# Mean square of x from each head's 32x32 matrix of v_m with itself, summed by VectorE's accumulating product, with another seed for the planner

## The chip, the cores and the metric

The kernel runs on one core of one Trainium2 chip. The metric is the device time of one execution in microseconds (us), as the median of the runs. A profiled execution gives the trace from which rows are quoted.

## The reference, cut to what matters

Three stages run one after the other on inputs of 4 batches, 8 heads, 576 positions and 64 columns per head: an attention through 32 memory slots per head, a gated feed-forward layer behind an RMS norm, and a second feed-forward layer.

```python
a = softmax(phi, axis=2)                              # over the 576 positions; phi: 4,8,576,32
k_m = einsum('bhsm,bhsd->bhmd', a, k)                 # 32x64 per head
v_m = einsum('bhsm,bhsd->bhmd', a, v)
attn = softmax(q @ k_m.T / 8, axis=-1)                # 576x32 per head
x = (attn @ v_m) with the heads side by side          # 2304 x 512
rms = sqrt(mean(x * x, axis=-1) + 1e-6)
xn = x / rms * rms_g
h = silu(xn @ w_gate) * (xn @ w_val)                  # d_ff 1536
x2 = h @ w_out
out = gate(x2 @ w_in) @ w_out2                        # d_ff 2048
```

q and k are 200 times their usual size, so the scores are far apart. The weights come as float64 and are converted to float32 on the chip.

## The kernel before, in words

The kernel never forms xn. It multiplies v_m (with the gains rms_g folded in, tile `vT`) into the gate and value weights, 128 rows of weights per chunk (`chunk`, `convert`, `vw`), and applies the scaled attention weights A = attn / rms to the product (`gv`). What it needs of x is only its mean square per token, for 1 / rms.

The attention part goes by batch and by pair of token blocks:

- `soft(b)` makes the exponentials of phi, `memory(b)` forms k_m and v_m of a batch on TensorE (tile `kvps`), divides by the sums (tiles `kd`, `vs`), transposes both into one PSUM bank (`kT`), and copies out `kmT` (ScalarE) and `vT` (VectorE).
- `spread_v(b)` lays v_m out as `vbd`: for each group of 4 heads a 128 x 256 matrix with the 32 x 64 block of each head on its diagonal.
- `pair(n)` runs 10 times: eight pairs of two blocks of 128 tokens (I = 2), and two rest pairs with 64 tokens of each of two batches (I = 1). It forms the scores (`sc`), the softmax (`mx`, `e`, `sm`), transposes the weights (`aTp`, copied to `aT`), multiplies them by `vbd` to get x itself in PSUM (`xp`, L844, one bank for each i), and ScalarE squares and sums x (`square`, L835). GpSimd turns the sum into 1 / rms (L856, L860) and scales the weights (L862), which are transposed (`ATp`, L870) and split into a high and a low part (`Ah`, `Al`, or in `late`).

Then `gv` makes the products with the weights (`gps`, `vps`, L984), `gate` the activation, `out1` the first layer's output (L1079), `quads` and `outs` the second layer (L1423, L1546).

The order of all instructions is fixed when the program is built. `Agenda` plays the kernel's generators against assumed costs (`yield "V", 0.45` is 0.45 us on VectorE), always starts what can start first, and breaks ties by priority. A `yield` with two engine letters lets it pick the engine that would end first: `"VAhi"` and `"VAsign"` in the weight conversion (VectorE or ScalarE), `"VGvbd"` in `spread_v` (VectorE or GpSimd). Costs are wobbled by up to 3% with a random generator that starts from `SEED`, so another seed gives another order throughout the program. `heat` puts idle matmuls of zeros (`heat`, L586) where TensorE would have nothing to do, until k_m of batch 3 is there.

Of the kernel before, what the change touches and what calls it, by code (L numbers as in the profile page):

```python
# [9 lines left out]
F32 = mybir.dt.float32  # L10
# [3 lines left out]
AF = mybir.ActivationFunctionType  # L14
ALU = mybir.AluOpType
AX = mybir.AxisListType
P = 128
# [8 lines left out]
BUFS = {"phi": 2, "kv": 2, "q": 2, "qr": 2, "pm": 1, "gm": 2, "s1": 2, "kd": 2, "qT": 2, "e": 4, "aT": 3, "half": 1, "raw": 4, "x": 2, "w": 2, "vw": 2, "ab": 3, "tx": 6, "w2s": 2, "wr": 8, "u": 6, "gs": 20, "gg": 6, "uo0": 5, "uo1": 5}  # L26
# [18 lines left out]
DUTY = {"Pm": 0.64, "Pw": 0.83, "Ps": 0.5}  # L45
W_AFTER = [("km", 0)]
WO1_AFTER = {(0, 0): ('gv', 8), (1, 0): ('gv', 12), (0, 1): ('gv', 9), (1, 1): ('gv', 12), (0, 2): ('gv', 10), (1, 2): ('gv', 12), (0, 3): ('gv', 11), (1, 3): ('gv', 12), (0, 4): ('gv', 12), (1, 4): ('gv', 12), (0, 5): ('gv', 13), (1, 5): ('gv', 12)}
BIAS = {"VAhi": -0.0664, "GAlow": -0.8, "VGlo": 0.3, "GVe": 0.8, "VGal": 0.3, "VAsign": 0.5, "VGvbd": -0.169, "VAgate": 0}
DMA_LAG = 1.8
D_HALF = 1.7  # L50
OVER = {"V": 0.085, "A": 0.1}
FETCH = (256, 63, 80.0, 6.1, 3.6, 80)
TICK = 3.413
SEED, WOBBLE = 4, 0.06
WARM = 1.38
P_SOFT, P_PAIR, P_CONV, P_VW, P_GV, P_OUT1, P_W2, P_F2 = 0, 100, 800, 102, 850, 900, 3000, 4000
P_W = 4004
# [9 lines left out]
class Agenda:  # L67
# [28 lines left out]
    def add(self, pri, stream):  # L96
        self.count += 1
        self._go([pri, self.count, stream, None, self.done, ""], None)
# [131 lines left out]
def tile_attn_moe(tc, q, k, v, phi, w_gate, w_val, w_out1, rms_g, w_in2, w_out2, out):  # L230
# [10 lines left out]
    nc = tc.nc  # L241
    B, H, S, D = q.shape
    M = phi.shape[3]
    DM = H * D
# [6 lines left out]
    HP = P // 2  # L251
# [5 lines left out]
    HM = H * M  # L257
# [21 lines left out]
    def bank(tag, name):  # L279

        early = BANKS.get(tag + "0") if "attention" not in agenda.flags else None
        z = yield "pick", early or BANKS[tag]
        return psum.tile([P, 512], F32, tag=f"b{z}", name=name), ("bank", z)
# [4 lines left out]
    mask, half, ones, power = consts[:, 0:4], consts[:, 4:5], consts[:, 5:6], consts[:, 6:8]  # L288
# [12 lines left out]
    vT = [keep.tile([P, KC, M], F32, name=f"vT{b}") for b in range(B)]  # L301
# [5 lines left out]
    add, mark = agenda.add, agenda.set  # L307
# [117 lines left out]
    st = pool(att, "st", "right")  # L425
# [1 line left out]
    rest, th_free, th_home = [], [], []  # L427
    qr_t = {}
    kmT_t = [st.tile([P, H, 2, M], F32, name=f"kmT{b}") for b in range(B)]
    vbd_t = [st.tile([P, 2, 4, D], F32, name=f"vbd{b}") for b in range(B)]  # L430
    gT = st.tile([P, KC], F32, name="gT")
    g4 = st.tile([KC, P], F32, name="g4")
    nc.scalar.dma_start(out=g4, in_=rms_g.rearrange("(c p) -> c p", p=P))
# [160 lines left out]
    def memory(b):  # L594
# [6 lines left out]
        for j in range(J):  # L601
            yield "Pm32", 0.22
            for g in range(2):
                gs = slice(HP * g, HP * g + HP)
# [56 lines left out]
                tp[:, P * g : P * g + P], kd[:, g].rearrange("p t d -> p (t d)"), ident  # L661
            )
        nc.tensor.transpose(tp[:, HM : HM + P], vs.rearrange("p g d -> p (g d)"), ident)
        add(P_SOFT + 2 * b + 1, spread_v(b, vs))
        kmT = kmT_t[b]
        for z in range(2):
            yield "A", 0.38
# [9 lines left out]
            out=vT[b], in0=tp[:, HM : HM + P].rearrange("p (c m) -> p c m", c=KC),  # L677
            in1=gT.unsqueeze(2).to_broadcast([P, KC, M]), op=ALU.mult,
        )
        yield "give", tp_bank  # L680
        mark(("vT", b))

    def spread_v(b, vs):
        vbd = vbd_t[b]
        for g in range(2):
            eng = yield "VGvbd", (0.41, 0.62)
            (nc.vector if eng == "V" else nc.gpsimd).tensor_tensor(
                out=vbd[:, g],
                in0=vs[:, g].unsqueeze(1).to_broadcast([P, 4, D]),
                in1=mask.unsqueeze(2).to_broadcast([P, 4, D]),  # L690
                op=ALU.mult,
            )
        mark(("vbd", b))
        yield "give", "kd"

    def used_q(b):
# [44 lines left out]
    def per_batch(pr):  # L741
        if pr[0] == B:
            return [(b, slice(HP * k, HP * k + HP)) for k, b in enumerate(RESTS[pr[1]])]
        return [(pr[0], slice(0, P))]

    def pair(n):
# [80 lines left out]
        nc.scalar.activation(out=aT, in_=tv, func=AF.Copy)  # L827
        yield "give", tp_bank
        for bb, _ in per_batch(pr):
            yield "flag", ("vbd", bb)  # L830
        ss = st.tile([P, I], F32, tag="ss", name=f"ss_{name}", bufs=BUFS["e"])

        def square(i, xp, x_bank):
            yield "A", 0.78
            nc.scalar.activation(out=xp, in_=xp, func=AF.Square, accum_out=ss[:, i : i + 1])  # L835
            yield "give", x_bank
            mark(("ss", pr, i))

        for i in range(I):
            xp, x_bank = yield from bank("x", f"xp_{name}_{i}")  # L840
            yield f"P{8 * len(per_batch(pr))}", 0.86
            for g in range(2):
                for bb, rows in per_batch(pr):
                    nc.tensor.matmul(  # L844
                        out=xp[rows, 256 * g : 256 * g + 256],
                        lhsT=aT[:, i, g, rows],
                        rhs=vbd_t[bb][:, g].rearrange("p h d -> p (h d)"),
                        start=True, stop=True, skip_group_check=True,
                    )
            add(pri, square(i, xp, x_bank))  # L850
        yield "give", "aT"
        for i in range(I):
            yield "flag", ("ss", pr, i)
        y = st.tile([P, I], F32, tag="y", name=f"y_{name}", bufs=BUFS["e"])
        yield "G", 0.3
        nc.gpsimd.tensor_scalar(  # L856
            out=y, in0=ss, scalar1=1.0 / DM, scalar2=1e-6, op0=ALU.mult, op1=ALU.add
        )
        yield "G", 0.72
        nc.gpsimd.tensor_tensor(out=y, in0=y, in1=power[:, 0:I], op=ALU.pow)  # L860
# [808 lines left out]
```

## Time and profile before

| | |
|---|---|
| median of the runs | 773.75 us |
| profiled execution | 773.81 us |
| its span, first to last instruction | 772.0 us |
| TensorE matmul busy | 759.0 us (98%) |
| VectorE (DVE) busy | 621.6 us (81%) |
| ScalarE (ACT) busy | 462.7 us (60%) |
| GpSimd (POOL) busy | 61.1 us (8%) |

Busy time is the union of an engine's instructions; the rest of the span the engine waits. "PEld" are TensorE's weight loads, which overlap its matmuls. A float32 matmul of the program is two matmul instructions in the trace. Shares over the whole span hide that the attention part, in the first 94 us, loads the engines quite differently from the rest.

### The profile page before, as it was taken

Reading aid. Unit: us, or ns where it says so; the run is one execution under the profiler, and the core shown is the slowest. Engines: PE = TensorE matmul, PEld = TensorE weight load, DVE = VectorE, ACT = ScalarE, POOL = GpSimd, SP = SyncE. Lnnn points to the kernel's source line nnn. Section 1 sums busy time; section 2 is a strip of 40 time slices with the busy share of each in tenths; the row PEclk is TensorE's granted clock in tenths of the full one; section 3 lists DMA queues with packets and bytes.
Section 4 is the critical chain, followed back from the end, with each engine's and each line's share of the span. In section 5 each row is a group of like instructions: output and inputs, shape, how many; then the busy total and the mean of one; then the engine's idle time right before and its main releaser. Section 6 shows DMA issues by size and latency. Waiting matters only on the chain.

```text
span 772.0 us, 17234 instructions
## 1 busy us (share of the span) xinstructions
PE 759.0 (98%) x6383; PEld 700.6 (91%) x6383; DVE 621.6 (81%) x1257; ACT 462.7 (60%) x959; POOL 61.1 (8%) x84
## 2 busy tenths in 40 slices
PE   8899999999999999999999999999999999999997
PEld 4678888889999888988899999999999999999997
DVE  5798889998877787756789889997789895589963
ACT  2688887755556555645566656564467463565552
POOL 1556610000001000000000000000000000000000
PEclk9999999999999999999999999999999999999999
DMA  9995535788779775599647999779888878757866
GB/s 343 377 385 160 199 111 188 258 275 270 253 237 305 251 248 187 205 324 324 208 168 219 326 305 305 252 249 318 293 251 262 296 241 258 254 182 251 270 217 209
DMA packets 113371, 197.49 MB, mean 256 GB/s; under 512 B 10372, under 2 KB 41096, under 8 KB 113288
## 3 DMA queue, kind: packets, MB, share of 16 engines
q1 hardware_dynamic: 112368, 194.88, 75.4%
q10 hardware_dynamic: 920, 1.51, 0.5%
q8 instruction: 51, 0.84, 0.4%
q14 instruction: 32, 0.26, 0.1%
HBM read 151.26 MB, written 45.09 MB: 254 GB/s over the span
## 4 chain that ended last, share of the span: by engine, by line
PE 92%; DVE 3%; DMA 2%; ACT 1%; issue 1%; ACTq 0%; SPq 0%; DVEq 0%
PE ops L1079 18%; PE acc_b L1546 17%; PE qb L1423 12%; PE gps L984 10%; PE vps L984 10%; PE qc L1423 6%; PE acc_c L1546 6%; PE qa L1423 3%; PE vwps L934 3%; PE xp L844 2%; DMA kv<-in_k_dram 1%; PE kvps L606 1%; PE sc L723 1%; PE qps L772 1%; DMA x1B<-x_d 1%
## 5 line engine op out<-in xcount | busy, mean ns | idle before, releaser
L1079 PE MATMUL ops<-ab,wo1h 128*128 128x512 f32 (+1 forms) x480 | 137.2, 371 | 0.5 <-ACT xs L1093 0.5
L1423 PE MATMUL qb<-xop,wr 128*128 128x384 f32 x576 | 111.7, 337 | 0.0
L1423 PEld LDWEIGHTS qb<-xop,wr 128*128 128x128 f32 x576 | 100.3, 187 | 0.9 <-DVE xop L1298 0.5
L1079 PEld LDWEIGHTS ops<-ab,wo1h 128*128 128x128 f32 x480 | 84.7, 189 | 15.8 <-issue 2.9
L1079 PE MATMUL ops<-ab,wo1l 128*128 128x512 f32 (+1 forms) x240 | 88.4, 368 | 0.0
L1546 PE MATMUL acc_b<-wor,gg_A 128*128 128x256 f32 x648 | 80.8, 280 | 1.0 <-ACT gg_A L1494 0.8
L1546 PEld LDWEIGHTS acc_b<-wor,gg_A 128*128 128x128 f32 x648 | 79.3, 188 | 1.3 <-ACT gg_A L1494 1.0
L1385 ACT ACTIVATE u<-qb 128x384 f32<-128x384 f32 x72 | 35.2, 489 | 49.7 <-PE qb L1423 49.1
L1423 PE MATMUL qc<-xop,wr 128*128 128x384 f32 x288 | 58.3, 337 | 0.0
L1546 PE MATMUL acc_c<-wor,gg_S 128*128 128x256 f32 x432 | 53.0, 279 | 0.0
L1079 PEld LDWEIGHTS ops<-ab,wo1l 128*128 128x128 f32 x240 | 45.2, 188 | 7.9
L1546 PEld LDWEIGHTS acc_c<-wor,gg_S 128*128 128x128 f32 x432 | 52.2, 188 | 0.0
L1546 PE MATMUL acc_b<-wor,gg_S 128*128 128x256 f32 x432 | 51.7, 279 | 0.0
L1546 PEld LDWEIGHTS acc_b<-wor,gg_S 128*128 128x128 f32 x432 | 51.3, 188 | 0.0
L1423 PEld LDWEIGHTS qc<-xop,wr 128*128 128x128 f32 x288 | 50.9, 187 | 0.0
L344 ACT ACTIVATE raw<-raw 128x512 uint32<-128x512 uint32 x68 | 45.3, 673 | 0.0
L1016 ACT ACTIVATE kvth<-gps 128x64 f32<-128x64 f32 (+2 forms) x101 | 28.9, 305 | 18.8 <-PE gps L984 18.5
L984 PE MATMUL gps<-late,vwh 128*128 128x288 f32 x192 | 39.6, 294 | 0.0
L984 PE MATMUL vps<-late,vwh 128*128 128x288 f32 x192 | 39.6, 294 | 0.0
L1050 ACT ACTIVATE ab<-kvth 128x512 fp32r<-128x512 f32 (+1 forms) x40 | 22.7, 566 | 26.1 <-PE ops L1079 26.1
L954 DVE TENSOR_TENSOR vwl<-vwps,vwh 128x512 fp32r<-128x512 f32 x48 | 32.3, 685 | 7.2 <-ACT vwh L952 6.9
L1494 ACT ACTIVATE gg_S<-gs 128x384 fp32r<-128x384 f32 x52 | 26.8, 522 | 17.5 <-PE acc_b L1546 8.5
(188 smaller groups left out, 1730.1 us busy)
## 6 DMA issues: line engine op xcount, KB each, us to landing
wr<-win_d SPq DMA_DIRECT2D x168, 256.0 KB, 4.0
wor<-wout_d SPq DMA_DIRECT2D x168, 256.0 KB, 3.3
raw<-in_moe_w_out_dram SPq DMA_DIRECT2D x28, 512.0 KB, 4.9
win_d<-wins SPq DMA_DIRECT2D x56, 256.0 KB, 2.8
wout_d<-wouts SPq DMA_DIRECT2D x56, 256.0 KB, 2.9
raw<-in_moe_w_in_dram SPq DMA_DIRECT2D x16, 512.0 KB, 4.9
raw<-in_moe_w_gate_dram SPq DMA_DIRECT2D x12, 512.0 KB, 4.8
raw<-in_moe_w_val_dram SPq DMA_DIRECT2D x12, 512.0 KB, 5.7
```

The costliest lines, as they stand in the source:

```text
L344: nc.scalar.activation(out=low, in_=low, func=AF.Copy, scale=LOW_SCALE, bias=LOW_BIAS)
L844: nc.tensor.matmul(out=xp[rows, 256 * g : 256 * g + 256], lhsT=aT[:, i, g, rows], rhs=vbd_t[bb][:, g].rearrange("p h d -> p (h d)"), start ...
L934: nc.tensor.matmul(out=vps[g][0][32 * c : 32 * c + 32, 2 * P * x : 2 * P * x + 2 * P], lhsT=vT[n // NF1 * 2 + x][hs, c, :], rhs=t[hs, c].r ...
L954: nc.vector.tensor_tensor(out=lv, in0=vps[g][0], in1=hv.bitcast(F32), op=ALU.subtract)
L984: nc.tensor.matmul(out=p[:, 0:HB], lhsT=wt[:, g, i, :], rhs=at[b][:, g, c], start=(g == 0 and y == 0), stop=(g == 1 and y == 2),)
L1016: nc.scalar.activation(out=t, in_=g[:, c], func=AF.Silu)
L1050: nc.scalar.activation(out=ah, in_=src, func=AF.Copy)
L1079: nc.tensor.matmul(out=p[:, 0:n], lhsT=wt[:, fc, d], rhs=at, start=(fc == 0 and x == 0), stop=(fc == NF1 - 1 and x == 2),)
L1385: nc.scalar.activation(out=u, in_=src, func=AF.Copy)
L1423: nc.tensor.matmul(out=bank, lhsT=wt[:, kc, :], rhs=xt[:, kc, :], start=(start and kc == 0 and i == 0), stop=(kc == 1 and i == 2), skip_gr ...
L1494: nc.scalar.activation(out=t[:, 0], in_=src, func=AF.Copy)
L1546: nc.tensor.matmul(out=acc[x + "001"[t]][:, t % 2], lhsT=g[:, gi, P * t : P * t + P], rhs=w[:, wi], start=((o, t) in FIRST and q == 0 and ...
```

## The change

The product with `vbd`, and the square of x, go. In their place `memory` copies the transposed v_m of a batch (`vsT`) out of PSUM on ScalarE, and `gram` multiplies it with itself: for each group of 4 heads a 128 x 128 matrix, of which a mask keeps the 32 x 32 block of each head (`gram_t`). `pair` multiplies the transposed weights by it (`zp`, 128 columns in place of 256, both i in one PSUM bank), and VectorE multiplies the result with the weights themselves, 256 columns for each i, and sums along the row (`accum_out`); the sum over d of x squared is a G a for G = v_m v_m'. GpSimd's first step clips at zero and adds 1e-6. `"VGvbd"` leaves the planner's list, and SEED goes from 4 to 12.

```diff
-BIAS = {"VAhi": -0.0664, ..., "VGvbd": -0.169, "VAgate": 0}
+BIAS = {"VAhi": -0.0664, ..., "VAgate": 0}
-SEED, WOBBLE = 4, 0.06
+SEED, WOBBLE = 12, 0.06
-    vbd_t = [st.tile([P, 2, 4, D], F32, name=f"vbd{b}") for b in range(B)]
+    gram_t = [st.tile([P, 2, 4, M], F32, name=f"gram{b}") for b in range(B)]
@@ memory
-        add(P_SOFT + 2 * b + 1, spread_v(b, vs))
...
+        mark(("vT", b))
+        yield "A", 0.25
+        vsT = st.tile([P, P], F32, tag="vsT", name=f"vsT{b}", bufs=BUFS["kd"])
+        nc.scalar.activation(out=vsT, in_=tp[:, HM : HM + P], func=AF.Copy)
         yield "give", tp_bank
-        mark(("vT", b))
+        add(P_SOFT + 2 * b + 1, gram(b, vsT))
-    def spread_v(b, vs):
...
+    def gram(b, vsT):
+        gp = []
         for g in range(2):
-            eng = yield "VGvbd", (0.41, 0.62)
-            (nc.vector if eng == "V" else nc.gpsimd).tensor_tensor(
-                out=vbd[:, g], in0=vs[:, g]..., in1=mask..., op=ALU.mult)
-        mark(("vbd", b))
+            gp.append((yield from bank("t", f"gramps{b}_{g}")))
+        yield "P8", 0.6
+        for g in range(2):
+            gs = slice(HP * g, HP * g + HP)
+            nc.tensor.matmul(out=gp[g][0][:, 0:P], lhsT=vsT[gs], rhs=vsT[gs], start=True, stop=True, ...)
+        for g in range(2):
+            yield "V", 0.29
+            nc.vector.tensor_tensor(
+                out=gram_t[b][:, g], in0=gp[g][0][:, 0:P].rearrange("p (h m) -> p h m", h=4),
+                in1=mask.unsqueeze(2).to_broadcast([P, 4, M]), op=ALU.mult)
+            yield "give", gp[g][1]
+        mark(("gram", b))
         yield "give", "kd"
@@ pair
-            yield "flag", ("vbd", bb)
+            yield "flag", ("gram", bb)
-        def square(i, xp, x_bank):
-            yield "A", 0.78
-            nc.scalar.activation(out=xp, in_=xp, func=AF.Square, accum_out=ss[:, i : i + 1])
-            yield "give", x_bank
-            mark(("ss", pr, i))
+        zp, z_bank = yield from bank("x", f"zp_{name}")
+        yield f"P{8 * I * len(per_batch(pr))}", 0.96 * w * len(per_batch(pr))
         for i in range(I):
-            xp, x_bank = yield from bank("x", f"xp_{name}_{i}")
-            yield f"P{8 * len(per_batch(pr))}", 0.86
             for g in range(2):
                 for bb, rows in per_batch(pr):
                     nc.tensor.matmul(
-                        out=xp[rows, 256 * g : 256 * g + 256],
+                        out=zp[rows, 256 * i + P * g : 256 * i + P * g + P],
                         lhsT=aT[:, i, g, rows],
-                        rhs=vbd_t[bb][:, g].rearrange("p h d -> p (h d)"),
+                        rhs=gram_t[bb][:, g].rearrange("p h m -> p (h m)"),
                         start=True, stop=True, skip_group_check=True)
-            add(pri, square(i, xp, x_bank))
         yield "give", "aT"
+        zv = zp[:, 0 : I * HM].rearrange("p (t n) -> p t n", t=I)
         for i in range(I):
-            yield "flag", ("ss", pr, i)
+            yield "V", 0.45
+            nc.vector.scalar_tensor_tensor(
+                out=zv[:, i], in0=zv[:, i], scalar=1.0 / DM, in1=ev[:, i],
+                op0=ALU.mult, op1=ALU.mult, accum_out=ss[:, i : i + 1])
+        yield "give", z_bank
-        yield "G", 0.3
-        ... scalar1=1.0 / DM, scalar2=1e-6, op0=ALU.mult, op1=ALU.add
+        yield "G", 0.4
+        ... scalar1=0.0, scalar2=1e-6, op0=ALU.max, op1=ALU.add
```

## Rows read from the trace of the kernel before

**Rows 1.** The page: busy time, share and instructions of each engine; the chain by engine.

```profile
PE 759.0 (98%) x6383; PEld 700.6 (91%) x6383; DVE 621.6 (81%) x1257; ACT 462.7 (60%) x959; POOL 61.1 (8%) x84
...
PE 92%; DVE 3%; DMA 2%; ACT 1%; issue 1%; ACTq 0%; SPq 0%; DVEq 0%
```

**Rows 2.** Busy time by stretch (us from the start; its length, then engines as headed).

```profile
core 0: us, PE busy (x) PEld busy (x) DVE busy (x) ACT busy (x) POOL busy (x), PEclk, DMA share, GB/s
...
28.00:88.00 60.00, 56.70 (x875) 46.06 (x874) 52.87 (x113) 53.22 (x116) 40.12 (x48) 1.00 0.75 260
88.00:330.00 242.00, 242.00 (x2126) 215.65 (x2125) 199.85 (x427) 153.09 (x353) 11.74 (x11) 1.00 0.69 236
330.00:690.00 360.00, 358.90 (x2293) 346.67 (x2292) 290.87 (x553) 208.64 (x402) 1.53 (x1) 1.00 0.81 267
690.00:768.20 78.20, 77.32 (x649) 76.94 (x647) 60.46 (x121) 38.81 (x78) 0.00 (x0) 1.00 0.74 235
```

**Rows 3.** Busy time by stretch of the zero matmuls at L586 alone (PE, PEld).

```profile
28.00:88.00 60.00, 1.14 (x3) 0.35 (x3) 1.00 0.75 260
```

**Rows 4.** Line 984, first gate product: min/median/max ns, first and last start.

```profile
L984 PE MATMUL gps<-Ah,vwh x96: 288/295/402, 65.9 to 189.5; 128*128 128x288 f32 x96
```

**Rows 5.** Instructions on tile `q`, loads to landing included.

```profile
L493 SPq DMA_DIRECT2D q<-in_q_dram x4: 373/679/2121, 2.3 to 43.8; - x4
...
DMA to landing us min/median/max: 9.8/12.8/13.0
```

**Rows 6.** Tile `xp`: its instructions, min/median/max ns, first and last start.

```profile
L844 PEld LDWEIGHTS xp<-vbd,aT x80: 133/190/192, 28.0 to 86.4; 128*128 128x128 f32 x64, 128*64 128x64 f32 x16
L844 PE MATMUL xp<-vbd,aT x80: 379/379/483, 28.1 to 86.6; 128*128 128x256 f32 x64, 128*64 128x256 f32 x16
L835 ACT ACTIVATE xp<-xp x18: 582/590/603, 29.2 to 87.5; 128x512 f32<-128x512 f32 x18
L835 ACT ACTIVATION_READ_ACCUMULATOR xp<-xp x18: 181/194/202, 29.7 to 88.0; 128x1 f32 x18
```

**Rows 7.** The chain that ended last: start us, us, what.

```profile
32.50 1.92 PE xp L844 x8
...
40.03 0.44 PE ATp L870 x4
...
60.92 1.01 PE xp L844 x8
...
759.64 8.49 PE acc_b L1546 x72
```

**Rows 8.** The page's costliest groups: a weight load of the last stage.

```profile
L1546 PEld LDWEIGHTS acc_b<-wor,gg_A 128*128 128x128 f32 x648 | 79.3, 188 | 1.3 <-ACT gg_A L1494 1.0
```

**Rows 9.** Busy time by stretch of the matmuls at L844 alone (PE).

```profile
28.00:65.90 37.90, 9.29 (x40) 1.00 0.89 315
```

**Rows 10.** Busy time over 36 to 54 us, the sum of three 6-us stretches.

```profile
sum 18.00, PE 16.27 PEld 12.84 DVE 17.42 ACT 15.38 POOL 11.55; mean PE 5.42 PEld 4.28 DVE 5.81 ACT 5.13 POOL 3.85
```

**Rows 11.** Groups by form, 0 to 110 us, ACT: a 128-column copy from PSUM.

```profile
L881 ACT ACTIVATE Ah<-ATp 128x128 fp32r<-128x128 f32 x2 | 0.5, 272 | 0.0
```

**Rows 12.** Groups by form, 0 to 110 us, DVE: busy us, mean ns; idle before.

```profile
L954 DVE TENSOR_TENSOR vwl<-vwps,vwh 128x512 fp32r<-128x512 f32 x10 | 6.7, 680 | 1.7 <-ACT vwh L952 1.5
L355 DVE SCALAR_TENSOR_TENSOR w<-raw,w 128x512 uint32<-128x512 uint32 x8 | 5.5, 692 | 0.0
...
L687 DVE TENSOR_TENSOR vbd<-vs,consts 128x256 f32<-128x256 f32 x6 | 3.0, 520 | 0.0
...
L341 DVE TENSOR_SCALAR w<-raw 128x512 f32<-128x512 f32 x4 | 2.3, 582 | 0.7 <-DMA raw<-in_moe_w_gate_dram 0.7
...
L676 DVE TENSOR_TENSOR vT<-kT,gT 128x128 f32<-128x128 f32 x4 | 1.1, 286 | 0.7 <-ACT kmT L669 0.7
...
L1024 DVE SCALAR_TENSOR_TENSOR kvth<-kvth,gps 128x288 f32<-128x288 f32 x1 | 0.4, 435 | 0.0
...
L1024 DVE SCALAR_TENSOR_TENSOR kvth<-kvth,gps 128x224 f32<-128x224 f32 x1 | 0.4, 373 | 0.0
```

More of the change, by code (lines that the diff above doesn't have):

```diff
@@ L47 @@
 WO1_AFTER = {(0, 0): ('gv', 8), (1, 0): ('gv', 12), (0, 1): ('gv', 9), (1, 1): ('gv', 12), (0, 2): ('gv', 10), (1, 2): ('gv', 12), (0, 3): ('gv', 11), (1, 3): ('gv', 12), (0, 4): ('gv', 12), (1, 4): ('gv', 12), (0, 5): ('gv', 13), (1, 5): ('gv', 12)}
-BIAS = {"VAhi": -0.0664, "GAlow": -0.8, "VGlo": 0.3, "GVe": 0.8, "VGal": 0.3, "VAsign": 0.5, "VGvbd": -0.169, "VAgate": 0}
+BIAS = {"VAhi": -0.0664, "GAlow": -0.8, "VGlo": 0.3, "GVe": 0.8, "VGal": 0.3, "VAsign": 0.5, "VAgate": 0}
 DMA_LAG = 1.8
@@ L679, in memory @@
         )
+        mark(("vT", b))
+        yield "A", 0.25
+        vsT = st.tile([P, P], F32, tag="vsT", name=f"vsT{b}", bufs=BUFS["kd"])
+        nc.scalar.activation(out=vsT, in_=tp[:, HM : HM + P], func=AF.Copy)
         yield "give", tp_bank
-        mark(("vT", b))
-    def spread_v(b, vs):
-        vbd = vbd_t[b]
+        add(P_SOFT + 2 * b + 1, gram(b, vsT))
+    def gram(b, vsT):
+        gp = []
         for g in range(2):
-            eng = yield "VGvbd", (0.41, 0.62)
-            (nc.vector if eng == "V" else nc.gpsimd).tensor_tensor(
[L688 to L691, printed above, removed]
-            )
-        mark(("vbd", b))
+            gp.append((yield from bank("t", f"gramps{b}_{g}")))
+        yield "P8", 0.6
+        for g in range(2):
+            gs = slice(HP * g, HP * g + HP)
+            nc.tensor.matmul(
+                out=gp[g][0][:, 0:P], lhsT=vsT[gs], rhs=vsT[gs],
+                start=True, stop=True, skip_group_check=True,
+            )
+        for g in range(2):
+            yield "V", 0.29
+            nc.vector.tensor_tensor(
+                out=gram_t[b][:, g], in0=gp[g][0][:, 0:P].rearrange("p (h m) -> p h m", h=4),
+                in1=mask.unsqueeze(2).to_broadcast([P, 4, M]), op=ALU.mult,
+            )
+            yield "give", gp[g][1]
+        mark(("gram", b))
         yield "give", "kd"
@@ L844, in pair @@
                     nc.tensor.matmul(
-                        out=xp[rows, 256 * g : 256 * g + 256],
+                        out=zp[rows, 256 * i + P * g : 256 * i + P * g + P],
                         lhsT=aT[:, i, g, rows],
-                        rhs=vbd_t[bb][:, g].rearrange("p h d -> p (h d)"),
+                        rhs=gram_t[bb][:, g].rearrange("p h m -> p (h m)"),
                         start=True, stop=True, skip_group_check=True,
                     )
-            add(pri, square(i, xp, x_bank))
         yield "give", "aT"
+        zv = zp[:, 0 : I * HM].rearrange("p (t n) -> p t n", t=I)
         for i in range(I):
-            yield "flag", ("ss", pr, i)
+            yield "V", 0.45
+            nc.vector.scalar_tensor_tensor(
+                out=zv[:, i], in0=zv[:, i], scalar=1.0 / DM, in1=ev[:, i], op0=ALU.mult, op1=ALU.mult,
+                accum_out=ss[:, i : i + 1],
+            )
+        yield "give", z_bank
         y = st.tile([P, I], F32, tag="y", name=f"y_{name}", bufs=BUFS["e"])
-        yield "G", 0.3
+        yield "G", 0.4
         nc.gpsimd.tensor_scalar(
-            out=y, in0=ss, scalar1=1.0 / DM, scalar2=1e-6, op0=ALU.mult, op1=ALU.add
+            out=y, in0=ss, scalar1=0.0, scalar2=1e-6, op0=ALU.max, op1=ALU.add
         )
```

## The prediction

> **What bounds the kernel now.** I read the page first. TensorE has a matmul in flight for 759.0 us of a 772.0 us span, and the chain that ended last is TensorE for 92% of its length [rows 1]. A change pays here if it takes work from TensorE at a place where TensorE's next work is ready. VectorE is second with 81%, but that is an average over stages, so I split the span.
>
> The view by stretches shows where the 13 us without matmuls lie [rows 2]. From 88 to 330 us TensorE never rests, from 330 to 690 us it rests 1.1 us, from 690 to its last matmul 0.9 us. So behind 88 us there are 2.0 us of slack in 680, and the last 3.8 us are the final addition and store. Ahead of that, from 28 to 88 us, TensorE is busy 56.7 of 60 us, VectorE 52.9 and ScalarE 53.2: the attention part loads three engines to about 90% each [rows 2]. Idle matmuls of zeros hide little of that stretch, 1.1 us [rows 3].
>
> Two rows say what can stand in for attention work. The first gate product starts at 65.9 us [rows 4]; from then on TensorE has large ready work. Before that it has nearly none but attention. The queries of the last batch are asked for at 43.8 us, and such a load takes 12.8 us to land [rows 5], so the last batch's pairs cannot begin before about 56.6 us however fast the others go.
>
> **The change on TensorE.** The x product is 80 matmul instructions, 64 with 128 output rows and 16 with 64, all of 256 columns, and all between 28 and 87 us [rows 6]. Spacing counts, not the 379 ns that one is in flight: the chain has 8 full ones in 1.92 us (0.24 each) and 8 of the rest pairs in 1.01 us (0.126 each) [rows 7]. Removed: 64 x 0.24 + 16 x 0.126 = 17.4 us.
>
> In their place come as many with 128 columns. No product of that shape is in the trace. The nearest are the transposes, 4 in 0.44 us, or 0.11 each [rows 7]; that is the lower bound, because a product's weight load is longer. The upper bound is a weight load that nothing hides, 0.19 [rows 6]. I take 0.12: the last stage has weight loads of the same 0.188 us [rows 8] and still passes 72 matmuls in 8.49 us, 0.118 each [rows 7]. With half of it for the rest pairs, the new product is 64 x 0.12 + 16 x 0.06 = 8.7 us, between 7.9 and 13.7.
>
> `gram` adds 4 batches x 2 groups x 2 = 16 instructions of 128 columns: at 0.11 that is 1.8 us, 0.9 if the two halves of the array overlap as the rest pairs' do, 3.0 with bare weight loads. TensorE's net: 17.4 - 8.7 - 1.8 = **6.9 us less work**, bounds 0.7 and 8.6.
>
> **Where that shows.** 40 of the 80 instructions start before 65.9 us [rows 9], so half the saving, 3.45 us, falls on each side. Behind 65.9 us ready gate products move up, and I count it in full. Its cover is that the weights for those gates are converted in time; without that it is worth 0. Before 65.9 us it can only help by bringing attention forward, with the last queries due at 56.6 us in any case: 0 to 3.45 us. From 36 to 54 us VectorE is the fuller engine, 17.42 of 18 us against TensorE's 16.27 [rows 10], so I take a third, nearer to 0: 1.1 us.
>
> **The change on ScalarE and VectorE.** ScalarE loses 18 squares of 0.590 and 18 reads of the accumulator of 0.194 [rows 6], 14.1 us, and gains 4 copies of 128 columns at 0.272 [rows 11], 1.1 us: 13.0 us less.
>
> VectorE gains 8 x 2 + 2 = 18 accumulating products of 256 columns. The same operation without the sum takes 0.373 us at 224 columns and 0.435 at 288 [rows 12], so 0.40 at 256. The trace has no sum on VectorE; ScalarE's costs a further 0.194 [rows 6]. Between 0.40 and 0.60 I take the middle, 0.50, there being one neighbour on each side: 9.0 us (7.3 to 10.7). Writing into PSUM is in these bounds; no row prices it apart. 8 mask products of 128 columns from PSUM at 0.286 add 2.3 us, and the 6 `vbd` products that VectorE had go, 3.0 us [rows 12]; the other 2 leave GpSimd. Net +8.3 us (6.6 to 10.0).
>
> For the sum there is a rule. The Trainium skill, "VectorE: DVE Perf Modes", section "Two Vector instructions with no wait between them", counts an operation that writes out its accumulator as two instructions; by it the upper end would hold, 18 x 0.60 = 10.7 us. No VectorE row here shows it.
>
> A second rule speaks against the change. An operation of this kind with two 4-byte sources in SBUF takes 0.692 us for 512 columns, and a plain two-source operation 0.680 [rows 12]: no sign of half speed. The Trainium skill, "Vector Engine (DVE) Microarchitecture Reference", section "Points that are easy to get wrong", says that such an operation with two non-bf16 SBUF sources runs at half throughput. By that, 256 columns would cost about 0.27 more each and the sum 4.8 us more; the row disagrees, and here one source is in PSUM.
>
> VectorE has 60 - 52.9 = 7.1 us free in that stretch, so 8.3 does not fit unless something moves. What can move are the weight conversions, on which the planner may choose: the sign step, 5.5 us, and the high part, 2.3 us [rows 12]. ScalarE has 60 - 53.2 + 13.0 = 19.8 us for them. In the forecast the planner moves 2 to 3 us of them and VectorE costs nothing on the path.
>
> **Small edits.** The new wait is for `gram`, with the pair's product queued behind it on TensorE. Its chain beyond the old one is a copy, two pairs of matmuls and two mask products, 0.27 + 0.44 + 0.57 = 1.3 us per batch. The pair's own softmax covers it: three VectorE passes of 512 columns, 0.68 each as at L954 [rows 12], and ScalarE's exponentials. Uncovered it costs at most 4 x 1.3 = 5.2 us. The bank of transposes and the `kd` slot are held longer by the same 1.3 us under the same cover, and `gram` takes two banks while the pair needs one fewer. No transfer is added or moved on any queue. GpSimd's clip is as wide as the step it replaces: 0.
>
> The seed redraws the order of everything. Behind 88 us it can give back at most the 2.0 us of slack [rows 2]; what it can take has no row, and I bound it by what this change gives. I count 0.
>
> **The sum.** The profiled execution took 773.81 us, 1.8 us around its span, and the median is 773.75, so they can be taken as one. 773.8 - 3.45 - 1.1 = **769.3 us**.
>
> **The rivals.**
> *VectorE becomes the bound (slower).* If the planner leaves the conversions where they are, 28 to 88 us holds 52.9 + 8.3 = 61.2 us of VectorE work. At the fullest share it held over 18 us, 17.42 / 18 = 97% [rows 10], that takes 63.1 us, and the weights for the first gates come 3.1 us late: 776.9 us. For it: the pairs' new products go ahead of conversions in priority, and VectorE stays at 83% up to 330 us. Against: ScalarE's 13 us. It decides once less than 3 us of conversion leave VectorE.
>
> *The new order eats the gain.* The old order leaves only 2.0 us of waits in 680 [rows 2], so another draw is likelier to add waits than to remove them. With 4 us more of them: 773.3 us. Against: the planner is the same and plans for TensorE.
>
> *More than forecast.* Attention before 65.9 us shortens with the full saving, at the lower bound for the products: 773.8 - 8.6 = 765.2 us. For it: each pair's path loses the squares, and ScalarE becomes light. Against: the last queries' landing and VectorE's 97%.
>
> *The clock.* It is granted at 1.00, the 2.4 GHz level, in every stretch from 28 us to the last matmul [rows 2], with TensorE busy. With 6.9 us less work in the attention part, one stretch there may fall to 1.2 GHz: 6 us of matmuls take 12 there, and I get 775.3 us. Against: zero matmuls fill gaps until late in attention. The Trainium skill, "TensorE: Matmul & The Clock Gate", section "Part 1: The HAM clock gate (the "warmup" mystery)", calls the low level the default, which activity lifts.
>
> **How the numbers follow.** Forecast 0.52 (its own range 766 to 772.5), VectorE 0.15, new order 0.17, more 0.13, clock 0.03. Predicted is the likeliest, 769.3. For 8 in 10 the range takes in all these centres, 765.2 to 776.9, and little more: 764.5 to 777. Two per cent, about what a measurement of this kernel can tell from no change, is 15.5 us: below 758.3 or above 789.2. No case is centred there; an excess of several bounds at once gets 0.02 on the fast side and 0.03 on the slow side.
>
> **What would show it.** Right: in the groups, the new product's 80 instructions at 0.11 to 0.13 us spacing; 18 VectorE products of 0.4 to 0.6 us; ScalarE about 13 us below 462.7; TensorE's total busy time 5 to 8 us lower, with rests of no more than 4 us behind 88 us. VectorE's rival: TensorE waits for weight products between 66 and 130 us. New order: rests behind 88 us well above 2.0 us. Clock: a granted clock below 1.00 before 90 us. The forecast is wrong if TensorE's work falls as worked out and its idle time grows by as much.

## The result and the profile after

The changed kernel took **778.57 us** (median of 5 runs, 775.97 to 780.91) against 773.75: a ratio of 1.0064, 95% interval [1.0052, 1.0076], so slower by 0.6%. The forecast was 769.3 us, its range 764.5 to 777. The profiled execution has a span of 776.8 us and a mean granted clock of 0.993, where before stands at 772.0 and 1.00.

The page after, busy time and the chain that ended last (answers to [rows 1]):

```profile
PE 758.0 (98%) x6397; PEld 702.1 (90%) x6397; DVE 623.1 (80%) x1286; ACT 459.9 (59%) x938; POOL 66.2 (9%) x88
...
PE 91%; DVE 4%; DMA 2%; issue 2%; ACT 1%; ACTq 0%; DVEq 0%
```

The stretches after (answers to [rows 2]; three finer ones behind the dots):

```profile
28.00:88.00 60.00, 52.05 (x879) 45.14 (x877) 54.28 (x137) 44.75 (x87) 38.88 (x46) 0.94 0.74 261
88.00:330.00 242.00, 240.82 (x2116) 213.74 (x2115) 198.29 (x428) 152.00 (x345) 18.66 (x19) 0.99 0.69 232
330.00:690.00 360.00, 358.57 (x2281) 345.97 (x2280) 290.26 (x551) 212.31 (x408) 1.53 (x1) 1.00 0.82 268
690.00:772.80 82.80, 82.00 (x681) 81.63 (x679) 62.78 (x125) 41.88 (x84) 0.00 (x0) 1.00 0.72 227
...
60.00:66.00 6.00, 3.03 (x150) 2.56 (x149) 5.84 (x11) 5.70 (x11) 4.40 (x7) 1.00 0.56 189
66.00:72.00 6.00, 6.00 (x40) 5.37 (x38) 5.93 (x17) 5.00 (x12) 4.01 (x3) 0.72 0.54 178
84.00:90.00 6.00, 4.22 (x34) 3.04 (x32) 5.61 (x19) 3.79 (x8) 3.60 (x5) 1.00 0.22 87
```

The reader is to see three things. From 28 to 88 us TensorE's busy time is 4.65 us below before, part of it at a lower clock; ScalarE's is 8.5 us below; VectorE's is 1.4 us above and fuller than TensorE's. From 66 to 72 us the clock is 0.72, so part of that window is at the 1.2 GHz level; in the window from 60 to 66 us TensorE had been busy 3.03 of 6 us. And the rests behind 88 us (1.18 + 1.43 + 0.80 = 3.4 us) are 1.4 us more than before.

**Where the time came in.** One row carries the case: the last transposes of the scaled weights (tile `ATp`), which end the attention part. The same row of the kernel before, and of after (engine, operation, count, min/median/max ns, first and last start in us):

```profile
L870 PE MATMUL ATp<-ident,e x36: 270/272/329, 38.5 to 93.1; 128*128 128x128 f32 x36
```

```profile
L880 PE MATMUL ATp<-ident,e x36: 270/273/475, 32.8 to 96.9; 128*128 128x128 f32 x36
```

From that row to the end of the span it is 772.0 - 93.1 = 678.9 us before and 776.8 - 96.9 = 679.9 after. So 3.8 of the span's 4.8 us were lost before attention ended, and 1.0 behind it.

The chain of waits after, in order of time, start and duration in us:

```profile
41.48 2.50 issue
43.99 0.82 PE sc L746 x21
...
60.77 2.13 PE kvps L606 x139
62.90 2.97 issue
65.87 0.42 PE kvps L606 x5
...
71.96 0.33 PE kT L663
72.29 0.91 PE zp L849 x8
73.20 0.37 DVE kvth L1034
...
73.85 0.40 DVE zp L859 x2
...
74.47 0.88 DVE zp L859 x4
75.34 0.56 DVE mx L803
75.90 0.40 DVE zp L859 x2
76.30 0.55 DVE e L809
...
82.68 1.06 PE gps L994 x6
```

It differs in two kinds of pieces: TensorE's waits for instructions (`issue`), 2.50 and 2.97 us where the longest before is 1.60, and behind 73.2 us a run of VectorE pieces in which the new sums (L859) stand among the softmax of the last pairs. The last transposes of batch 3's memory (tile `kT`) start at 71.96 us. Before, that part of the chain is TensorE's:

```profile
67.58 1.06 PE xp L844 x4
...
68.86 1.89 PE xp L844 x8
70.74 1.08 PE sc L723 x32
71.83 1.06 PE xp L844 x4
```

The memory of batch 3 itself starts at 57.4 us before and 60.7 after, its last products at 59.4 and 66.0 (the wait of 2.97 us lies between), the transposes at 64.6 and 71.96.

The new work itself, by tile:

```profile
L849 PE MATMUL zp<-gram,aT x80: 272/275/417, 27.9 to 89.1; 128*128 128x128 f32 x64, 128*64 128x128 f32 x16
L859 DVE SCALAR_TENSOR_TENSOR zp<-zp,e x18: 407/430/475, 29.1 to 89.8; 128x256 f32<-128x256 f32 x18
L859 DVE DVE_READ_ACCUMULATOR zp<-zp,e x18: 135/142/151, 29.4 to 90.1; 128x1 f32 x18
```

### The profile page after: what moved, and what is told of

Its sections match the earlier page's. It is cut to its first block, busy times and chain, and to the rows that moved or that the text cites. A ratio compares the mean times of both kernels' runs of the same rounds, so it can differ in the third digit from the quotient of the medians.

```text
span 776.8 us, 17275 instructions
## 1 busy us (share of the span) xinstructions
PE 758.0 (98%) x6397; PEld 702.1 (90%) x6397; DVE 623.1 (80%) x1286; ACT 459.9 (59%) x938; POOL 66.2 (9%) x88
## 4 chain that ended last, share of the span: by engine, by line
PE 91%; DVE 4%; DMA 2%; issue 2%; ACT 1%; ACTq 0%; DVEq 0%
PE ops L1089 18%; PE acc_b L1556 16%; PE qb L1433 12%; PE gps L994 9%; PE vps L994 9%; PE acc_c L1556 7%; PE qc L1433 6%; PE vwps L944 3%; PE qa L1433 3%; PE kvps L606 1%; DMA kv<-in_k_dram 1%; PE qps L784 1%; PE zp L849 1%; DMA win_d<-wins 1%; PE sc L735 1%
## 5 line engine op out<-in xcount | busy, mean ns | idle before, releaser
L1433 PEld LDWEIGHTS qb<-xop,wr 128*128 128x128 f32 x576 | 100.6, 187 | 0.7 <-ACT u L1395 0.3
L344 ACT ACTIVATE raw<-raw 128x512 uint32<-128x512 uint32 x65 | 43.5, 673 | 0.0
L962 ACT ACTIVATE vwh<-vwps 128x512 fp32r<-128x512 f32 x48 | 27.8, 594 | 20.2 <-PE vwps L944 20.1
L1041 DVE TENSOR_TENSOR kvth<-kvth,vps 128x64 f32<-128x64 f32 (+2 forms) x100 | 30.6, 321 | 9.3 <-PE vps L994 8.8
```

The source lines that it names most:

```text
L344: nc.scalar.activation(out=low, in_=low, func=AF.Copy, scale=LOW_SCALE, bias=LOW_BIAS)
L962: nc.scalar.activation(out=hv, in_=vps[g][0], func=AF.Copy)
L1041: nc.vector.tensor_tensor(out=t, in0=t, in1=v[:, c], op=ALU.mult)
L1433: nc.tensor.matmul(out=bank, lhsT=wt[:, kc, :], rhs=xt[:, kc, :], start=(start and kc == 0 and i == 0), stop=(kc == 1 and i == 2), skip_gr ...
```

## The experiments

Two numbers sort the 18 experiments and the two kernels: the time, and the start of the last `ATp`. In all 20 profiles the span is 676.6 to 681.4 us behind that start, so whatever is done to attention reaches the end, up to some 2.5 us that the later order takes or gives.

| run | us | ratio to before, 95% | last ATp, us | clock |
|---|---|---|---|---|
| before, seed 4 | 773.7 | 1 | 93.1 | 1.000 |
| before, seed 9 (e16) | 776.46 | [1.0023, 1.0051] | 98.9 | 1.000 |
| before, seed 3 (e10) | 779.57 | [1.0061, 1.0091] | 97.7 | 0.998 |
| before, seed 2 (e8) | 781.27 | [1.0078, 1.0108] | 97.7 | 1.000 |
| after, seed 9 (e17) | 776.0 | [1.0020, 1.0064] | 95.5 | 0.998 |
| after, seed 12 | 778.57 | [1.0052, 1.0076] | 96.9 | 0.993 |
| after, seed 2 (e11) | 780.33 | [1.0069, 1.0099] | 99.5 | 0.993 |
| after, seed 4 (e2) | 781.91 | [1.0098, 1.0128] | 101.9 | 0.993 |
| after, seed 1 (e9) | 783.32 | [1.0095, 1.0139] | 100.2 | 0.988 |
| before, half product (e4) | 772.95 | [0.9982, 1.0003] | 92.2 | 0.998 |
| before, short square (e15) | 773.46 | [0.9990, 1.0009] | 92.7 | 0.999 |
| before, extra sum (e7) | 778.05 | [1.0033, 1.0071] | 98.0 | 0.998 |
| before, whole trade (e14) | 776.08 | [1.0016, 1.0042] | 95.4 | 0.998 |
| after, short sum (e6) | 776.47 | [1.0023, 1.0046] | 94.7 | 0.994 |
| after, wide product (e3) | 781.08 | [1.0080, 1.0113] | 100.6 | 0.996 |
| after, shifted blocks (e5) | 778.32 | [1.0049, 1.0079] | 97.8 | 0.991 |
| after, filled rests (e18) | 777.57 | [1.0038, 1.0064] | 96.3 | 0.999 |
| after, low parts on GpSimd (e12) | 776.10 | [1.0024, 1.0055] | 96.4 | 0.993 |
| the same, high parts on ScalarE, seed 7 (e13) | 778.79 | [1.0037, 1.0075] | 99.8 | 0.993 |
| e12 with filled rests (e19) | 776.02 | [1.0022, 1.0041] | 96.1 | 1.000 |

The clock is that of the profiled execution. In the quotes theory I is the supply of TensorE's instructions, theory II the new seed's order alone, theories III and V are VectorE's time, and theory O is the order of TensorE's instructions with its waits. The second gate chunk starts with the 49th gate product, at 90.1 us before and 93.45 after.

**The seed alone.** One line, in the kernel before (e8, e10, e16) and in the changed one (e2, e9, e11, e17):

```diff
-SEED, WOBBLE = 4, 0.06
+SEED, WOBBLE = 2, 0.06
```

> The changed kernel with the planner's old seed, 4, and nothing else. Theory I (TensorE gets its instructions in blocks of 256, and an order that empties a block faster than the next one comes makes it wait, behind the longest waits at half its clock): the result follows from the waits named issue and from the granted clock; span = 763.5 us (the spans of both kernels less their issue waits, their lost clock time and, for the one before, the 6.9 us of matmul work saved give 762.5 and 764.4) + issue waits of TensorE + lost clock time, within 2 us. Theory II (it is the new seed's order alone that lost the gain): with the old seed the forecast comes true, 769 us or less, clock 1.00. Theory III (VectorE's added 8 us set the pace): 777 us or more with any seed, with TensorE waiting for VectorE rather than for its instructions.

> The kernel before with another seed (2 for 4), nothing else. If the seed of before was a lucky draw and the changed kernel's is an ordinary one, this comes at 776 to 781 us with the second gate chunk at 92 to 96 us. If the change itself costs the time, it comes at 772.5 to 775 us.

> The changed kernel with another seed (1 for 12). If the change itself costs the time, 777 to 782 us as with seeds 12 and 4, and the transposes of batch 3 behind 70 us again. If it is the draw, some seed should fall at 770 to 774 us with the transposes of batch 3 at 63 to 66 us; one seed can miss that.

> The kernel before with a third seed (3 for 4), nothing else. If seed 4 is simply a good draw and other seeds are like seed 2 (781.3 us), 776 to 782 us. If seed 2 was the exception, 773 to 775 us; the cost of the changed kernel would then be the change's own.

> The changed kernel with a fourth seed (2), the one with which the kernel before took 781.3 us. If the change is worth nothing beside the draw, 778 to 783 us, like seeds 12, 4 and 1. If TensorE's saved 6.9 us came through at an equal draw, 772 to 776 us.

> The kernel before with a fourth seed (9), the one that comes nearest to seed 4 in the planner's own play. If the play ranks the draws, 773 to 777 us; if it does not, 778 to 782 us like seeds 2 and 3.

> The changed kernel with seed 9, in the planner's own play level with seed 12. If the play ranks the draws, 776 to 780 us; if the change has no cost of its own, some draw of it must come down to 773 to 775 us, and this is the likeliest of those left.

The kernel before with three other seeds is 2.7, 5.9 and 7.3 us slower than with seed 4 (each against the runs of before on its own chip), without any other edit: seed 4 is a good draw. At equal seeds the changed kernel's median stands 0.5 us lower (9), 0.9 lower (2) and 8.2 higher (4). With seeds 9 and 2 the two kernels don't differ by more than their intervals. (The generator gives a number for each step of the play, so the same seed is not the same order in both kernels.) So the draw is as large as what the two kernels differ by. Theory II falls: the changed kernel with seed 4 takes 781.91 us, where theory II had 769 or less. With seed 2 before, batch 3 shows the draw. The last transposes of its memory start at 71.0 us there, against 64.6 with seed 4:

```profile
L663 PE MATMUL kT<-ident,vs x4: 272/273/273, 16.4 to 71.0; 128*128 128x128 f32 x4
```

The clock is 1.000 there, so it has no part in that lateness. Batch 3 is not all that a draw does: the changed kernel with seed 2 has these transposes at 68.4 us and takes 780.33, with seed 9 at 70.5 and takes 776.0. Seed 12 was not run in the kernel before.

**TensorE's work alone.** Half of the product's columns go in the kernel before, its order kept (e4, 8.6 us less work); in the changed kernel 64 of the 80 product instructions get their 256 columns back (e3):

```diff
-                        out=xp[rows, 256 * g : 256 * g + 256],
+                        out=xp[rows, 256 * g : 256 * g + P],
...
```

> The kernel before, in its own order, with the x product cut from 256 to 128 columns (half of the columns of x are left out of the mean square; the squares still take 512 columns, each read twice, and go to SBUF). It takes 8.6 us of matmul time out and adds nothing to VectorE. Theory I: the part behind 65.9 us pays, 4.3 us, the part before it turns into waits for instructions: about 769 us, issue waits up by 1 to 2 us from 2.6. Theories II and III, under which TensorE's own time counts in full: 765 us.

> The changed kernel in its own order, with three of four products by the 128-column matrix made 256 columns long (the second half is a copy that the next product overwrites). It gives TensorE back 5 to 6 us of work, half of it ahead of 66 us. Theory I: the part ahead of 66 us goes into the waits for instructions and costs little, the part behind costs up to 3 us, and the fuller TensorE may save a drop of its clock behind 82 us, 1.7 us: 777 to 781.5 us. Theory III: VectorE sets the pace, so no change, 778.6 us. If TensorE's work counted in full: 784 us.

e4 brings 0.5 us against its before (773.42), with an interval that holds no change. Its 10 runs fall apart by clock: four at 1.000 take 771.87 to 772.05 us, six at 0.995 to 0.998 take 772.88 to 774.74. TensorE's saved time is worth at most some 1.5 us, and most of the runs, those at a lower clock, don't show even that. No theory had this: they said 769 and 765 us. The chain of e4 says where the time went. From 42.4 to 86.7 us it now goes through VectorE and ScalarE, but for one piece of TensorE's (0.67 us of transposes) and one of GpSimd's (1.06 us), though attention ends only 0.9 us earlier:

```profile
68.02 1.22 DVE w L350 x2
...
71.45 0.61 DVE mx L792
72.15 0.69 DVE e L798
...
79.22 0.68 ACT sq L836 x2
79.92 0.69 ACT sq L836 x2
...
86.74 1.07 PE vps L989 x6
```

So ahead of the end of attention there were several chains of nearly one length, and with TensorE's shortened the others set the end. e3 shows that more work is not free: 2.5 us for the 5 to 6 us that were expected of it, where theory III, VectorE alone, had no change.

**VectorE's work alone**, added to before as 18 sums from constants (e7), taken from after by summing 32 columns (e6):

```diff
+            nc.vector.scalar_tensor_tensor(
+                out=xs[:, 512:768], in0=xs[:, 0:256], scalar=1.0 / DM, in1=xs[:, 256:512],
+                op0=ALU.mult, op1=ALU.mult, accum_out=xa,
+            )
...
```

```diff
-                out=zv[:, i], in0=zv[:, i], scalar=1.0 / DM, in1=ev[:, i], op0=ALU.mult, op1=ALU.mult,
+                out=zv[:, i, 0:32], in0=zv[:, i, 0:32], scalar=1.0 / DM, in1=ev[:, i, 0:32], op0=ALU.mult, op1=ALU.mult,
```

> The kernel before in its own order, with an extra accumulating product of 256 columns on VectorE at each of the 18 squares (from constants to scratch, nobody waits for it; some 0.57 us each, 10 us in all). Theory V: the work cannot be hidden, the second gate chunk starts later than 90.1 us by 3 us or more, 776.5 to 779 us. Theory O: VectorE has room by waits that move, at most 1.5 us more, 773.5 to 775 us.

> The changed kernel in its own order, with VectorE's accumulating product over 32 of the 256 columns (it leaves out the rest of the sum, so the values are not the reference's). This takes some 0.3 us from each of 18 instructions on VectorE, about 5.5 us in all between 28 and 93 us, and nothing from TensorE or ScalarE. Theory V (VectorE's work ahead of the last batch's memory and of the first gate chunk is what delays the changed kernel): the transposes of batch 3 (at 72.0 us) and the second gate chunk (at 93.4 us) come 2 to 4 us earlier, 775 us. Theory O (the order of the instructions on TensorE, and its stalls on new instruction blocks, hold it back): 778 to 779 us, no milestone moves by over 1 us.

The sums of e7, on which nothing waits, and those of e6:

```profile
L853 DVE SCALAR_TENSOR_TENSOR xs<-xs x18: 361/414/1528, 27.9 to 90.2; 128x256 f32<-128x256 f32 x18
L853 DVE DVE_READ_ACCUMULATOR xs<-xs x18: 75/79/83, 28.2 to 90.5; 128x1 f32 x18
```

```profile
L859 DVE SCALAR_TENSOR_TENSOR zp<-zp,e x18: 175/192/233, 29.0 to 89.1; 128x32 f32<-128x32 f32 x18
```

By the medians, 18 x (0.414 + 0.079) = 8.9 us of VectorE's time cost 4.1 us (778.05 against 773.96); with its few long ones, up to 1.53 us, the added work is 11.65 us. 18 x (0.430 - 0.192) = 4.3 us less gave 2.1 us back. Both ways a microsecond of VectorE in this part is worth a third to a half of a microsecond of the end, in two quite different orders. Theory O, by which no milestone moves, falls: the second gate chunk went from 90.1 to 94.95 us (e7) and from 93.45 to 91.25 (e6), the last `ATp` from 93.1 to 98.0 and from 96.9 to 94.7. Theory V holds for these and misses one: in e6 the transposes of batch 3 stay at 71.9 us, so shorter sums do not bring them forward.

**ScalarE's work alone** (e15), the square over 64 of 512 columns:

```diff
-            nc.scalar.activation(out=xp, in_=xp, func=AF.Square, accum_out=ss[:, i : i + 1])
+            nc.scalar.activation(out=xp[:, 0:64], in_=xp[:, 0:64], func=AF.Square, accum_out=ss[:, i : i + 1])
```

> The kernel before in its own order, with ScalarE's square over 64 of the 512 columns (it leaves out the rest of the sum). Takes some 0.45 us from each of 18 instructions on ScalarE, 8 us in all. If ScalarE's time in this stage is part of what sets the end, 770.5 to 772.5 us. If not, 773 to 774.5 us.

773.46 us: no gain. In this order, with TensorE's work in place, ScalarE's time was not what attention waits for.

**The whole trade in the old order** (e14), the sum in the place of ScalarE's square:

```diff
-            nc.scalar.activation(out=xp, in_=xp, func=AF.Square, accum_out=ss[:, i : i + 1])
+            nc.vector.scalar_tensor_tensor(
+                out=xp[:, 0:256], in0=xp[:, 0:256], scalar=1.0 / DM, in1=ev[:, i], op0=ALU.mult, op1=ALU.mult,
+                accum_out=ss[:, i : i + 1],
+            )
...
-                        out=xp[rows, 256 * g : 256 * g + 256],
+                        out=xp[rows, P * g : P * g + P],
...
```

> The kernel before in its own order (seed 4), with the trade of the change in place: the product of 128 columns in place of 256, no square on ScalarE, and where ScalarE's square stood an accumulating product of 256 columns on VectorE with the softmax weights (the matrix is still half of the old one, so the values are not the reference's). If the change itself costs what the runs of before and after differ by, 777.5 to 779.5 us. If the draw does, 772 to 775 us. VectorE's extra product in this order (778.05 us) with nothing given back by the other two would be 777 to 778 us.

776.08 us, 2.4 us over its before, between the two theories. TensorE from 28 to 88 us holds 5.9 us less than in [rows 2], VectorE 2.9 us more, and attention ends 2.3 us later:

```profile
28.00:88.00 60.00, 50.84 (x861) 42.14 (x859) 55.78 (x144) 42.42 (x80) 37.91 (x47) 0.97 0.75 261
```

So with no new draw the trade costs about 2.4 us, in this one order, which was planned for the old kernel; at seeds 9 and 2, with an order planned for each, it cost nothing that can be told. The sums take 18 x (0.423 + 0.141) = 10.2 us here. At e7's price by the medians, 0.46 us a microsecond, they would cost 4.7 us, so by this estimate the work that left TensorE and ScalarE together gave some 2.3 us back. Both savings without the sum were not run. `vbd` is still spread in it and `gram` not made, 2.4 us of VectorE against 2.2, nearly the same. What is left of the changed kernel's 4.8 us, another 2.4, I put to the draw; that is a difference of runs, not shown by a run of its own, and it holds whatever the longer waits for instructions cost.

**Instruction blocks and clock.** e5 replaces the first 40 idle matmuls by 10 longer ones, which moves the places where TensorE waits for its next instructions. e18 puts eight idle float32 matmuls where TensorE rested ahead of its low-clock stretches; e19 does so in e12:

```diff
+            if (b, j) == (3, 0):
+                fill(kvp[0][0], 3)
...
+        if pr == (B, 0):
+            fill(sfull, 3)
...
+        if pr == (B, 1):
+            fill(zp, 2)
...
```

> The changed kernel in its own order, with the first 40 matmuls of zeros replaced by 10 in float32 that take about as long: some 40 TensorE instructions fewer ahead of the attention part, so every block of 256 ends about 40 instructions later in the same order. Theory I: the waits named issue stand at other matmuls, their sum falls from 7.0 to about 5.5 us with none above 2.3 us, the clock drops once instead of three times, and the time falls to 774 us (772 to 776). Theories II and III: same order, same VectorE work, so 778.6 us within 1, and the waits stay at the same two matmul groups (the rest pair's scores and k_m of batch 3).

> The changed kernel in its own order with eight more idle float32 matmuls of zeros, 512 columns each: three ahead of the first rest pair's scores (the wait of 2.5 us at 41.5 us), three ahead of the memory of batch 3 (the wait of 3.0 us at 62.9 us) and two ahead of the last rest pair's product (the waits at 87 to 90 us). They are 16 matmul instructions, some 0.45 us each, 7 us more work on TensorE in places where it rested about 8 us. Clock theory: the low-clock stretches at 45.7, 66.2 and 90.1 us go or shrink, mean clock 0.997 or more, 775 to 777 us. Against it: the added work is itself late, clock or not, 779 to 782 us.

> The same eight idle matmuls in the changed kernel with the low parts turned to GpSimd (776.1 us without them, at clocks of 0.990 to 0.995). If the clock returns to 0.998 or more and the matmuls fill only rests, 773 to 775 us, level with the kernel before. If they delay the attention work, 777 to 780 us.

e5 gives 778.32 us: theory I's gain does not come, though its waits did as theory I had it (the long ones are 2.3 and 1.9 us, the second at other matmuls); the clock did not (0.991). Over repeated runs of one kernel the time often goes with the clock: e13 takes 775.96 and 776.26 us at 1.000 and 0.999, 780.35 and 780.76 at 0.993. It doesn't always: e17 takes 777.94 us at 0.994 and 780.42 at 0.996. But e18, which gets the clock back, tells how much of that can be had. Its stretches, the second and third where the changed kernel had 0.72:

```profile
28.00:88.00 60.00, 55.01 (x892) 44.51 (x890) 54.35 (x139) 45.20 (x87) 38.62 (x45) 1.00 0.76 261
...
66.00:72.00 6.00, 4.63 (x51) 3.91 (x51) 5.93 (x16) 5.77 (x13) 4.01 (x3) 1.00 0.56 171
...
90.00:96.00 6.00, 6.00 (x72) 5.03 (x72) 3.56 (x12) 2.84 (x8) 4.37 (x7) 1.00 0.89 287
```

All five runs are at 0.999 or 1.000, the matmuls' longest wait for instructions is down from 2.97 to 1.0 us, and the time is 777.57 us, 1.0 below the changed kernel and with an interval that overlaps its own. From 66 to 72 us TensorE now rests 1.4 us while VectorE is busy 5.93 of 6, as in the changed kernel, and the chain there is VectorE's:

```profile
67.04 1.49 DVE w L350
...
69.84 1.64 DVE w L350
71.48 0.14 DVE vs L663
...
71.67 0.53 PE kT L671 x2
```

The division of batch 3's memory (`vs`), for which its transposes wait, stands behind steps of the weight conversion (L350). e19 is level with e12, at a clock of 1.000 for 0.993. So most of the loss is not the clock's; where the clock comes back, TensorE waits for VectorE instead. What the idle matmuls themselves cost is not separated from what the clock gave back. What the waits for instructions cost stays open too: e5 only moves them, and e18 fills the long one with idle matmuls, so that batch 3's memory has its last products at 66.2 us, for 66.0 without. Why repeated runs of one kernel spread with the clock by up to 5 us, when a full clock brings only 1, stays open: the clock and the time may both follow from how early data or instructions come in.

**Settings that should beat both.** VectorE's low parts go to GpSimd (e12), and besides the high parts to ScalarE with seed 7 (e13):

```diff
-"VGlo": 0.3
+"VGlo": -0.3
```

> The changed kernel, seed 12, with the planner's bias for the low parts of the first weights turned from VectorE to GpSimd (VGlo 0.3 to -0.3). Meant to give VectorE back the time that its accumulating product takes, which the shortened sum showed to be worth some 2 us. If VectorE's time is what counts, the second gate chunk starts by 90 us and the time is 772 to 775 us. If the order that the planner draws counts for more, anywhere from 775 to 782 us.

> The changed kernel with the low parts turned to GpSimd and the high parts to ScalarE (VGlo -0.3, VAhi -0.5) and seed 7, the earliest end in the planner's own play among the settings tried. If the play ranks orders rightly and VectorE counts, 771 to 775 us, level with the kernel before or below it. If not, 776 to 782 us.

e13 has the high parts turned as well (VAhi -0.0664 to -0.5). e12 gains some 2 us on the changed kernel, with an interval that just overlaps its own; VectorE's busy time from 28 to 88 us falls by 1.6 us, and the second gate chunk starts at 92.9 us and not by 90. e13 gains nothing. No version of the changed kernel that was run beats 773.7 us; the best, 776.0, are e17, e19 and e12.

## Why the prediction was wrong

**"Behind 65.9 us ready gate products move up, and I count it in full."** This step failed, with the 1.1 us ahead of it; the two are the whole of the forecast's gain, 4.5 us. No gate product moved up. From 28 to 88 us TensorE passed 44 of them before and 42 after (their line alone, busy PE and PEld):

```profile
28.00:88.00 60.00, 7.23 (x44) 6.16 (x45) 1.00 0.75 260
```

```profile
28.00:88.00 60.00, 6.83 (x42) 5.73 (x42) 0.94 0.74 261
```

e4, with 8.6 us less work in the old order, passed 48; four more at 0.13 us each are 0.5 us, as much as it gained, within its uncertainty. The cover that the prediction named, weights converted in time, is not what is seen to fail: between 66 and 130 us no matmul of the changed kernel waits for a weight product (`vwh`, `vwl`). They wait 3.0 us for instructions and 0.5 to 0.7 us in all for each of the softmax (`e`, twice), the transposed weights `aT` and a gate step (`kvth`). What failed is the premise that TensorE's time sets when they can run. The span ends some 679 us behind the end of attention, and attention ends by chains in which VectorE's and ScalarE's pieces can stand for TensorE's, as e4 shows: TensorE's busy share there, 56.7 of 60 us [rows 2], measured how full it was, not what the pairs wait for.

**"VectorE costs nothing on the path."** Failed too, and it gives the sign. The conversions did move, by as much as the forecast had it: from 28 to 94 us VectorE has 5 sign steps for 8 (4.3 us for 5.5) and two high parts for four (0.8 us for 2.3), 2.7 us in all. Even so each microsecond of the sums cost a third to a half (e6, e7). The rival was to decide once less than 3 us of conversion left VectorE; 2.7 left, and it decided, so the forecast's own 2 to 3 us should already have had a price. The rival's 776.9 us came nearest to the result of all cases; 0.15 was too little. It had the engine, not the path: its sign, TensorE waiting for weight products between 66 and 130 us, did not come. Nor is it only the sum's place in the pair's chain, between the product and the scaling of the weights: e7's sums, for which nothing waits, cost as much.

**"The seed redraws the order ... I count 0."** Failed: a term put at nothing, with a bound that no row gave. The draw is worth 2.7 to 7.3 us against seed 4 in the kernel before, and the old order was a good draw. The argument for the rival was there, only 2.0 us of waits in 680, but it priced rests behind 88 us; the time was lost ahead of that. In the changed kernel one place is batch 3, whose transposes come at 71.96 us for 64.6: 3.3 us of it is the later start of its memory, 3.0 the wait for instructions, some 0.8 the longer way over VectorE from the last products to the transposes. How much of that reaches the end is not shown.

**The clock (0.03).** It happened: 0.94 from 28 to 88 us. With the clock back, e18 gains 1.0 us of the 4.8, against the 6 us that I gave it.

**What held.** The product's spacing: 8 in 0.91 us, 0.114 each, within 0.11 to 0.13. VectorE's sum: 0.430 + 0.142 = 0.57 us, within 0.40 to 0.60 and near its upper end. The Trainium skill, "VectorE: DVE Perf Modes", section "Two Vector instructions with no wait between them", counts two instructions for it; the trace agrees, with a second one of 0.142 us for the accumulator. The mask products: 0.281 for 0.286. One sum is off by a rounding: 64 x 0.12 + 16 x 0.06 is 8.64, not 8.7, and the net is 7.0 us. ScalarE is 8.5 us lower from 28 to 88 us, but only 2.8 over the whole span, not 13: VectorE's whole busy time rose by 1.5 us and not by 8, so conversions went from one to the other throughout. TensorE's whole busy time fell 1.0 us and not 5 to 8. In part that is the clock, for one in flight at the low clock lasts longer (the product's longest 417 ns, 275 in the median); but e4, at 0.998 and with 8.6 us less, fell by 3.9 us only, and the rest is open. Rests behind 88 us, 3.4, stayed below the 4 named. The prediction gave 0.95 to a change within 2%, and that is what came.

## What to carry to other kernels

Ask of the stage, not of the engine that is busiest: find the row where the stage ends, and what its chain would go through if the work you take were gone. Where three engines are each near 90% busy, several chains are nearly as long. Work taken from TensorE or ScalarE alone gave at most 0.5 us in the old order (e4, e15); VectorE's was worth a third to a half of its time both ways (e6, e7), and work added to TensorE cost about as much (e3). In a kernel whose order is drawn by a seeded planner, compare several draws of both versions before an edit is given a sign, and keep one order by hand (edit the instruction, not the plan) to price the edit alone.

## What the runs showed of the hardware

- TensorE's long waits for instructions come at fixed places of its program. Counting its matmuls, weight loads and semaphore waits in the trace together, they stand behind 705, 1217 and 1473 of them in both kernels and behind 2241 in the changed one: each number leaves 193 when divided by 256. A queue of the page brings the instructions; after:

```profile
q8 instruction: 51, 0.84, 0.4%
```

  That is 16 KB for each of 51 packets. From 15 to 42 us they come 6.1 to 6.9 us apart after, and an engine that uses up 256 instructions sooner has to wait: the memory of batch 3 is 288 short instructions, of which 278 pass in 2.2 us, and its last ones came 2.97 us late.
- An accumulating product on VectorE reads its accumulator in an instruction of its own: 0.142 us behind a product that reads and writes PSUM, 0.079 behind one from SBUF to SBUF (e7), with 0.430 and 0.414 us for the products.
- A less busy TensorE lost clock with the order unchanged: e4, with 8.6 us less work, ran at 0.995 to 0.998 in 6 of 10 runs, the kernel before at 0.999 or 1.000.
- A VectorE step beside a GpSimd instruction can take more than twice as long. None of the 104 L350 steps of the changed kernel with no GpSimd instruction beside them takes over 0.70 us; of the ten with one beside them for over 0.1 us, six take 0.71 to 1.72. Two of these lie ahead of the division of batch 3's memory (VectorE, then GpSimd; start and us):

```profile
66.71 1.57 DVE L350 SCALAR_TENSOR_TENSOR w<-w,raw 128x512 uint32<-128x512 uint32 x1
...
69.53 1.72 DVE L350 SCALAR_TENSOR_TENSOR w<-w,raw 128x512 uint32<-128x512 uint32 x1
```

```profile
66.69 1.05 POOL L827 TENSOR_TENSOR e<-e,sm 128x512 f32<-128x512 f32 x1 [2.29 <-DVE sm L825]
...
67.69 3.01 POOL L362 TENSOR_TENSOR w<-w,raw 128x512 f32<-128x512 f32 x2
```
